# Turning the projected x with transposing DMAs instead of on TensorE, in a three-layer float32 kernel

## The chip, the cores and the metric

The kernel runs on one core of one Trainium2 chip. The metric is device microseconds (us) of one execution; the median of two runs of the kernel before is 728.64 us. PE is TensorE (matrix products), DVE is VectorE, ACT is ScalarE, POOL is GpSimd, SP is the engine that issues most DMAs.

## The reference

Three layers follow each other on 4 batches of 448 rows and 768 channels (12 heads of 64):

```
attn = sigmoid(q @ k.T / 8 - log(448)) @ v                 # per head
gate = sigmoid(causal 5-tap convolution of attn, by channel)
x    = (gate * (attn @ w_val)) @ w_out
h    = relu(x.T @ w_tok1) @ w_tok2                          # mixes rows, 448 -> 256 -> 448
u    = x + h.T
out  = u + relu(u @ w_ch1) @ w_ch2                          # 768 -> 1536 -> 768
```

All of it is float32. The weights come as words of 64 bits (float64), which the kernel takes apart into a high and a low float32 part.

## The kernel before

**Numbers.** PE multiplies in a rounded float32 format. A matrix operand is therefore split into a high part (a rounding copy, on ACT) and a low part (the difference, on DVE), and each product is three: high by high, low by high, high by low. A *round* is 18 such products of 448 columns, six operand tiles by three.

**Stages.** First attention, for all 24 head pairs (`lead`), with the decoding of the first weights between (`dec_*`). Then the four batches, each in the steps that `dense_steps` lists: six *value rounds* (`pj(0, j)`: x by `w_val`; then the gate, and the split into `gv`), the *output stage* with six *output rounds* (`pj(1, j)`: `gv` by `w_out`, copied to `x2T`), and the token mixing. Token mixing needs x with rows on the partitions, but `x2T` has channels there: `transp(j)` turns the tile of 128 channels with four products by the identity (line 363, 448 rows being three and a half blocks of 128; the last 64 rows are doubled by line 355), and lines 365 to 368 split the result into `x2`. Three turned tiles make a half. `tok1(half, t)` (a *first token step*, 11 products) multiplies a half by `w_tok1`, `tok2(j)` (a *second token step*, 6 products) by `w_tok2`, adds x and stores u to `uscr` in HBM. Last the *channel stage*: four tiles of columns by twelve pieces of the hidden layer; `ch1(t, fc)` makes one piece (18 products into `psh`), `ch2` adds it into six accumulators (`pso`).

**Order.** The program is written in the order in which the engines' queues get it. `weave(steps, ops, share)` walks through PE's steps, which carry weights (products), and puts other work (`ops`) between them in proportion. The ops are: convolutions of the next batch (`post_ops`, which also reload x from `xscr` with `x_back`, on SP's queue, into four buffers), and the decoding of channel weights (`ch_ops`: eight steps for a piece, of DVE and ACT in turn, on loads by SP). Channel weights 2, 3 and 4 (`PRE`) are decoded early and parked in `wscr`; 0 and 1 are decoded in the last batch; 5 to 11 on DVE when the channel stage begins (`dec_ch`). Each engine works through its own queue in order; a waiting instruction holds up all that stand behind it.

**PSUM.** Projections, turned tiles and token steps share six tiles of one bank each (`psw`).

Of the kernel before, what the change touches and what calls it, by code (L numbers as in the profile page):

```python
# [12 lines left out]
U32 = mybir.dt.uint32  # L13
AF = mybir.ActivationFunctionType
# [4 lines left out]
PRE = (2, 3, 4)  # L19
CHAN_LOW = 600  # L20
OS_SHARE = 0.95
# [5 lines left out]
AHEAD = 5  # L27
SHIFT = 16
# [3 lines left out]
def tile_kernel(ctx, tc, qT, kT, v, w_val, conv_w, w_out, w_tok1, w_tok2, w_ch1, w_ch2, out):  # L32
# [69 lines left out]
    def decode_ops(pool, n, raw, h_out, l_out, sum_out=None, bufs=2):  # L102
        w = raw[:, : 2 * n].rearrange("p (n t) -> p n t", t=2)
        lo, hi = w[:, :, 0], w[:, :, 1]
        t = {}

        def first():
            t["a"] = pool.tile([P, DC], I32, tag="dec_a", bufs=bufs, name="dec_a")[:, :n]
            nc.vector.tensor_scalar(out=t["a"], in0=hi, scalar1=0x7FFFFE00, scalar2=None, op0=ALU.bitwise_and)  # L109
# [4 lines left out]
        def rest():  # L114
            t["c"] = pool.tile([P, DC], I32, tag="dec_c", bufs=1, name="dec_c")[:, :n]
            nc.vector.tensor_scalar(out=t["c"], in0=hi, scalar1=0x1FF, scalar2=None, op0=ALU.bitwise_and)
# [11 lines left out]
        def power():  # L128
            t["e"] = pool.tile([P, DC], I32, tag="dec_c", bufs=1, name="dec_e")[:, :n]
            nc.vector.tensor_scalar(out=t["e"], in0=t["a"], scalar1=-0x800000, scalar2=None, op0=ALU.bitwise_and)  # L130
# [11 lines left out]

        return [first, rebase, rest, join, sign, power, low, high]
# [148 lines left out]
    def x_back(i):  # L292
        x = xbp.tile([P, PAD + S], F32, tag="xb", bufs=4, name="xb")
        nc.gpsimd.memset(x[:, :PAD], 0.0)
# [30 lines left out]
    def dense_steps(b):  # L325
        gv, x2T, x2, h1 = {}, {}, {}, {}
        cur = {}

        def proj(sel, j, part):
# [16 lines left out]
            if sel == 0:  # L346
# [4 lines left out]
                split(gv[j][:, 0], gv[j][:, 1], g)  # L351
            else:
                x2T[j] = dn["late"].tile([P, 512], F32, tag="x2T", bufs=KD, name="x2T")
                nc.scalar.activation(out=x2T[j][:, :S], in_=ps[:, :S], func=AF.Copy)
                nc.vector.tensor_copy(x2T[j][:, S:], x2T[j][:, R0:S])

        def transp(j):
# [9 lines left out]
            nc.vector.tensor_tensor(  # L367
                out=x[REM:, NF], in0=pt[REM:, NF], in1=f(x[REM:, NF]), op=ALU.subtract
# [15 lines left out]
        def tok2(j):  # L384
# [11 lines left out]
            u = x2T[j][:, :S]  # L396
            nc.vector.tensor_tensor(out=u, in0=ps[:, :S], in1=u, op=ALU.add)
            nc.gpsimd.dma_start(uscr[b, j], u)

        def pj(sel, j):  # L400
            return [(12, lambda part=part: proj(sel, j, part)) for part in range(3)]

        def tr(j):
            return [(4, lambda: transp(j))]
# [8 lines left out]
        if b + 1 == B:  # L413

            outs = pj(1, 0) + pj(1, 1) + tr(0) + pj(1, 2) + tr(1) + pj(1, 3) + tr(2) + pj(1, 4) + pj(1, 5)

            outs = outs[: -len(pj(1, 5))]
            now = pj(1, 5) + t1(0, 0) + t1(0, 1) + tr(3) + tr(4) + tr(5)
            outs += [s + (True,) for s in now] + t2(0) + t2(1) + t2(2)
            return val, outs, t1(1, 0) + t1(1, 1) + [(18, lambda: ch1(0, 0))], t2(3) + t2(4) + t2(5)  # L420
        first = pj(1, 0) + pj(1, 1)
        if b == 0:

            first[2:4] = first[3], first[2]
# [114 lines left out]
    def post_ops(b):  # L539
        ops, gates = [], []  # L540
        for i in range(b * NP, (b + 1) * NP):
            parts = {}

            def first(i=i, parts=parts):
                parts["all"] = post_parts(i)
                parts["all"][0][0]()
                parts["all"][1]()

            ops.append(first)
            for t in range(1, KW):  # L550
                ops.append(lambda t=t, parts=parts: parts["all"][0][t]())
                if t == 2:
                    ops += gates
                    gates = [lambda parts=parts: parts["all"][3]()]

            def end(i=i, parts=parts):
                parts["all"][2]()
                if i + 4 < NPT:
                    x_back(i + 4)

            ops.append(end)
        return ops + gates
# [37 lines left out]
    def ch_parts(pool, fc, which, raw):  # L600
        if fc in PRE:
            to = [pool.tile([P, DM], F32R, tag=f"pre{a}", bufs=1, name="pre") for a in range(2)]
            ops = decode_ops(pool, DM, raw, *to, bufs=1)
# [9 lines left out]
        return decode_ops(pool, DM, raw, *wch[fc][which], bufs=1)  # L613
# [59 lines left out]
    def ch1(t, fc, lo=0, hi=KD):  # L673
# [12 lines left out]
        if (t, fc) == (0, 0):  # L686
# [24 lines left out]
    with tc.manual_schedule():  # L711
# [22 lines left out]
        back1, back2 = [], []  # L734
        for b in range(B):
            val, outs, t1, t2 = dense_steps(b)
            if b:

                weave(val[0] + back1 + sum(val[1:], []) + back2, first.pop(0), 0.95)
            else:  # L740
                val = sum(val, [])
                for n in (12, 8, 4):
                    val.insert(n, (0, dec_step))
# [7 lines left out]
            if b + 1 < B:  # L751
                weave(outs, post_ops(b + 1))
            else:
                os = outs + t1 + t2
            back1, back2 = t1, t2
            if b + 2 == B:
                pre.release()
                xbp.release()
                rp["a"] = tc.alloc_tile_pool(name="p2a", bufs=1, side="left")
                wch_alloc(rp["a"], 0)  # L760
# [82 lines left out]
```

## Time and profile before

| | |
|---|---|
| median of 2 runs | 728.64 us (728.64 to 728.65) |
| profiled execution, its own time | 728.47 us |
| its span, first to last instruction | 726.6 us |
| PE busy | 720.5 us, 99% of the span |
| DVE, ACT, POOL busy | 398.6, 256.4, 40.3 us |
| attention stage | until about 133 us |
| four batches | about 133 to 385 us |
| channel stage | about 385 to 726 us |

The share of an engine is a mean over stages: DVE is busy 55% of the span, but almost without a break in the output stages of the batches, where it does the convolutions of the next batch. Products are pipelined on PE, so the time of one (0.27 to 0.39 us) is longer than the step from one to the next (0.17 to 0.23); the chain of waits, which adds up in order of time, gives the second. A wait that another engine's row names is one on which the engine stood still; idle time of an engine that nobody waits for costs nothing.

### The profile page before, as it was taken

The numbers are of one execution on the slowest core, as the hardware profiler recorded it, in microseconds if no ns is written. First come the engines' busy times: TensorE is split into PE (matmuls) and PEld (weight loads), VectorE is DVE, ScalarE is ACT, GpSimd is POOL, SyncE is SP. The second block draws the span as 40 slices with busy tenths as digits, with TensorE's granted clock in tenths as the row PEclk, the third lists the DMA queues.
The fourth block names the chain that finished last, engine by engine and source line by source line (L and its number), as shares of the span: only waits on it lengthen the run. The fifth ranks groups of instructions, "written<-read, shape, count | busy, mean of one in ns | idle before, by whom it ended". The sixth has DMA issues, their size and how long they took to land.

```text
span 726.6 us, 10824 instructions
## 1 busy us (share of the span) xinstructions
PE 720.5 (99%) x4360; PEld 594.0 (82%) x4360; DVE 398.6 (55%) x690; ACT 256.4 (35%) x379; POOL 40.3 (6%) x90
## 2 busy tenths in 40 slices
PE   8999999999999999999999999999999999999998
PEld 3444444799999999999998888888888999999997
DVE  1799766489889879965577999220101400040002
ACT  5899888344333433422343443200001100020000
POOL 0001010000101111002012000000000000000000
PEclk9999999999999999999999999999999999999999
DMA  9747997221244233045827553240000600042001
GB/s 295 252 150 236 269 299 225 103 88 51 88 155 159 77 123 116 16 142 154 287 83 252 170 161 107 84 157 0 1 1 0 212 28 0 1 132 65 1 1 65
DMA packets 56737, 87.24 MB, mean 120 GB/s; under 512 B 8032, under 2 KB 48240, under 8 KB 56688
## 3 DMA queue, kind: packets, MB, share of 16 engines
q1 hardware_dynamic: 50352, 62.86, 28.0%
q0 software_dynamic: 5904, 23.23, 9.0%
q8 instruction: 34, 0.56, 0.3%
q10 hardware_dynamic: 432, 0.46, 0.2%
q14 instruction: 15, 0.12, 0.1%
HBM read 66.68 MB, written 19.86 MB: 119 GB/s over the span
## 4 chain that ended last, share of the span: by engine, by line
PE 91%; DVE 6%; ACT 1%; issue 1%; DMA 1%; SPq 0%; ACTq 0%
PE psh L680 24%; PE pso L701 24%; PE psd L340 18%; PE psy L277 8%; PE pss L262 8%; PE pst L380 4%; PE pst L393 3%; DVE gate L310 2%; PE pst L363 1%; DMA k<-kT 1%; ACT gv L87 0%; DVE dec_a L124 0%; DVE gate L349 0%; ACT ga L264 0%; DVE xs L318 0%
## 5 line engine op out<-in xcount | busy, mean ns | idle before, releaser
L89 DVE SCALAR_TENSOR_TENSOR r<-psh,r 128x384 fp32r<-128x384 f32 (+1 forms) x47 | 29.2, 621 | 214.5 <-ACT r L87 214.5
L680 PE MATMUL psh<-us,wch 128*128 128x512 f32 (+1 forms) x648 | 135.5, 362 | 0.0
L701 PE MATMUL pso<-r,wch 128*128 128x384 f32 (+1 forms) x630 | 131.1, 361 | 0.0
L680 PEld LDWEIGHTS psh<-us,wch 128*128 128x128 f32 x648 | 117.3, 188 | 12.7
L701 PEld LDWEIGHTS pso<-r,wch 128*128 128x128 f32 x630 | 113.8, 188 | 11.9
L87 ACT ACTIVATE r<-psh 128x384 fp32r<-128x384 f32 (+1 forms) x47 | 25.5, 542 | 231.6 <-PE psh L680 224.5
L340 PE MATMUL psd<-gv,wo 128*128 128x448 f32 x432 | 90.7, 365 | 0.0
L264 ACT ACTIVATE ga<-pss,bias_s 128x896 f32<-128x896 f32 x84 | 83.5, 1004 | 19.6 <-PE pss L262 18.9
L340 PE MATMUL psd<-xs,w 128*128 128x448 f32 x432 | 87.7, 362 | 0.1
L340 PEld LDWEIGHTS psd<-xs,w 128*128 128x128 f32 x432 | 80.8, 187 | 6.4 <-issue 0.7
L340 PEld LDWEIGHTS psd<-gv,wo 128*128 128x128 f32 x432 | 80.1, 188 | 5.1
L262 PE MATMUL pss<-q,k 64*64 64x448 f32 x672 | 78.6, 539 | 1.2 <-DMA k<-kT 0.7
L277 PE MATMUL psy<-ga,v 64*64 64x448 f32 x672 | 77.5, 536 | 0.0
L310 DVE SCALAR_TENSOR_TENSOR gate<-xb,cw,gate 128x448 f32<-128x448 f32 x96 | 65.7, 684 | 2.8
L262 PEld LDWEIGHTS pss<-q,k 64*64 64x64 f32 x672 | 26.2, 134 | 39.7 <-issue 29.2
L277 PEld LDWEIGHTS psy<-ga,v 64*64 64x64 f32 x672 | 25.7, 133 | 37.4 <-issue 35.9
L112 ACT ACTIVATE dec_a<-dec_a,exp_b 128x768 int32<-128x768 int32 (+3 forms) x43 | 36.8, 866 | 36.4 <-DVE dec_a L109 36.4
L124 DVE SCALAR_TENSOR_TENSOR dec_a<-raw,dec_a 128x768 int32<-128x768 int32 (+2 forms) x42 | 37.3, 888 | 19.6 <-ACT dec_a L112 19.6
L680 PE MATMUL psh<-us,w 128*128 128x512 f32 (+1 forms) x216 | 45.2, 362 | 0.0
L701 PE MATMUL pso<-r,w 128*128 128x512 f32 (+1 forms) x216 | 45.1, 362 | 0.0
L680 PEld LDWEIGHTS psh<-us,w 128*128 128x128 f32 x216 | 39.1, 188 | 4.3
L701 PEld LDWEIGHTS pso<-r,w 128*128 128x128 f32 x216 | 39.1, 188 | 4.2
(80 smaller groups left out, 648.0 us busy)
## 6 DMA issues: line engine op xcount, KB each, us to landing
raw<-w_ch SPq DMA_DIRECT2D x24, 768.0 KB, 4.3
v<-v SPq DMA_DIRECT2D x24, 224.0 KB, 5.9
uscr<-x2T POOLq DMA_DIRECT2D x24, 224.0 KB, 3.5
q<-qT SPq DMA_DIRECT2D x23, 224.0 KB, 3.9
k<-kT SPq DMA_DIRECT2D x22, 224.0 KB, 4.2
raw<-w_out POOLq DMA_DIRECT2D x6, 768.0 KB, 7.5
wscr<-pre POOLq DMA_DIRECT2D x12, 384.0 KB, 3.5
xscr<-xb SPq DMA_DIRECT2D x18, 224.0 KB, 4.4
```

Of the source, the lines that this page charges most:

```text
L87: nc.scalar.activation(out=h_out, in_=src, func=AF.Relu if relu else AF.Copy)
L89: nc.vector.scalar_tensor_tensor(out=l_out, in0=src, scalar=0.0, in1=f(h_out), op0=ALU.max, op1=ALU.subtract)
L112: nc.scalar.activation(out=t["a"], in_=t["a"], func=AF.Relu, scale=8.0, bias=exp_b)
L124: nc.vector.scalar_tensor_tensor(out=t["a"], in0=hi, scalar=-0x80000000, in1=t["a"], op0=ALU.bitwise_and, op1=ALU.bitwise_or)
L262: nc.tensor.matmul(ps[cols, j, :S], k[rows, keys], q[rows], start=True, stop=True)
L264: nc.scalar.activation(out=a, in_=ps[:, :, :S], func=AF.Sigmoid, bias=bias_s, scale=QK_SCALE)
L277: nc.tensor.matmul(y_t[i + h][cols, :S], v_t[i][rows, c, cols], a[rows, j], start=c == 0, stop=c == NB - 1)
L310: nc.vector.scalar_tensor_tensor(out=acc, in0=x[:, t : t + S], scalar=w, in1=acc, op0=ALU.mult, op1=ALU.add)
L340: nc.tensor.matmul(ps[:, :S], w(a, kk), s[:, c, :], start=kk == 0 and n == 0, stop=kk == KD - 1 and n == 2,)
L380: nc.tensor.matmul(ps[:, :HALF], a, x[:, m], start=n == 0, stop=n == len(mm) - 1)
L680: nc.tensor.matmul(ps[:, :n_t], wch[fc][0][a][:, kk * P : (kk + 1) * P], us_t[t, kk][:, c, :], start=kk == 0 and n == 0, stop=kk == KD - 1 ...
L701: nc.tensor.matmul(acc[j][:, :n_t], wch[fc][1][a][:, j * P : (j + 1) * P], r[c], start=fc == 0 and n == 0, stop=fc == KF - 1 and n == 2,)
```

## The change

- **Turning.** `transp` and its products go. `planes(j)` takes the 16-bit halves of each word of `x2T` apart with a copy on ACT, doubles the last 64 rows with a second one, and issues a transposing DMA on SP's queue, 128 x 1024 elements of 2 bytes from `pl` (three buffers) to `st` (one buffer). `join(j)` puts the halves together again with a copy on POOL, back into `pl`. `part2(j)` makes the high part in `x2` on ACT, `part3(j)` the low part on DVE. These four are steps of their own with weight 0, one to three rounds apart.
- **Token steps.** They move back: in the first three batches the three second token steps of the first half and both first token steps of the second half now stand behind the second value round of the next batch, one second token step behind its value rounds and the other two between its first output rounds. In the last batch two channel steps `ch1(0, 0)` and `ch1(0, 1)` stand among them, which write into two tiles of `wo`.
- **Gated values.** The low part (`low_gv`) is a step behind the third part of its value round, with room for another op between.
- **Convolutions** of the last two tiles of a batch go from the output stage to the next batch's value stage. The zeros ahead of a reloaded x are set by DVE, not POOL, and the reload stands two steps later.
- **Weights.** `PRE` is (2, 3); weight 4 is decoded with 5 to 11. Decoding uses the target or the raw data for its temporary values. Weights 0 and 1 are decoded from the last batch's value stage on, the loads of u and of weights 2 and 3 stand elsewhere in its steps.

```diff
-PRE = (2, 3, 4)
+PRE = (2, 3)
-OS_SHARE = 0.95
+OS_SHARE = 0.9
+EARLY = 2
+LATE = 2
...
-    def dense_steps(b):
+    def dense_steps(b, carry):
...
-                split(gv[j][:, 0], gv[j][:, 1], g)
+                nc.scalar.activation(out=gv[j][:, 0], in_=g, func=AF.Copy)
+                wait[j] = g
             else:
-                x2T[j] = dn["late"].tile([P, 512], F32, tag="x2T", bufs=KD, name="x2T")
-                nc.scalar.activation(out=x2T[j][:, :S], in_=ps[:, :S], func=AF.Copy)
-                nc.vector.tensor_copy(x2T[j][:, S:], x2T[j][:, R0:S])
-
-        def transp(j):
+                x2T[j] = dn["late"].tile([P, S], F32, tag="x2T", bufs=KD, name="x2T")
+                nc.scalar.activation(out=x2T[j], in_=ps[:, :S], func=AF.Copy)
+
+        def planes(j):
+            pl = dn["late"].tile([P, 2, 512], U16, tag="pl", bufs=3, name="pl")
+            st = dn["late"].tile([P, 2, NF + 1, P], U16, tag="st", bufs=1, name="st")
+            turn[j] = pl, st
+            nc.scalar.activation(
+                out=pl[:, :, :S], in_=x2T[j].bitcast(U16).rearrange("p (s h) -> p h s", h=2), func=AF.Copy
+            )
+            nc.scalar.activation(out=pl[:, :, S:], in_=pl[:, :, R0:S], func=AF.Copy)
+            nc.sync.dma_start_transpose(st.rearrange("p h c d -> p (h c) d"), pl.rearrange("p h s -> p (h s)"))
+
+        def join(j):
+            pl, st = turn[j]
+            back = pl.rearrange("p a b -> p (a b)")
+            nc.gpsimd.tensor_copy(back.rearrange("p (n h) -> p h n", h=2), st.rearrange("p h c d -> p h (c d)"))
+            turn[j] = back.bitcast(F32).rearrange("p (c d) -> p c d", c=NF + 1)
+
+        def part2(j):
...
-            pt = pd["pool"].tile([P, NF + 1, P], F32, tag="d", bufs=pd["n"], name="pst")
-            for c in range(NF + 1):
-                nc.tensor.transpose(pt[:, c], x2T[j][:, c * P : (c + 1) * P], ident)
             x = x2[half][:, :, jj * P : (jj + 1) * P]
-            nc.scalar.activation(out=x[:, : NF + 1], in_=pt, func=AF.Copy)
-            nc.vector.tensor_tensor(out=x[:, NF + 1 :], in0=pt[:, :NF], in1=f(x[:, :NF]), op=ALU.subtract)
+            nc.scalar.activation(out=x[:, : NF + 1], in_=turn[j], func=AF.Copy)
+
+        def part3(j):
...
+            raw = turn.pop(j)
+            nc.vector.tensor_tensor(out=x[:, NF + 1 :], in0=raw[:, :NF], in1=f(x[:, :NF]), op=ALU.subtract)
...
+        def low_gv(j):
+            nc.vector.tensor_tensor(out=gv[j][:, 1], in0=wait.pop(j), in1=f(gv[j][:, 0]), op=ALU.subtract)
...
-        outs = first + tr(0) + pj(1, 2) + tr(1) + pj(1, 3) + tr(2) + pj(1, 4)
-        outs += t1(0, 0) + t1(0, 1) + pj(1, 5) + tr(3) + t2(0) + tr(4) + t2(1) + tr(5) + t2(2)
-        return val, outs, t1(1, 0) + t1(1, 1), t2(3) + t2(4) + t2(5)
+        first = pj(1, 0) + tr(planes, 0) + pj(1, 1)
+        if b == 0:
+
+            first[2:5] = first[4], first[2], first[3]
+        def out(j, then):
+            steps = pj(1, j)
+            return steps[:1] + then + steps[1:]
+
+        outs = first + tr(planes, 1) + tr(join, 0) + carry[0]
+        outs += pj(1, 2) + tr(planes, 2) + tr(join, 1) + tr(part2, 0) + carry[1]
+        outs += out(3, tr(part3, 0)) + tr(planes, 3) + tr(join, 2) + tr(part2, 1)
+        outs += out(4, tr(part3, 1)) + tr(planes, 4) + tr(join, 3) + tr(part2, 2)
+        outs += out(5, tr(part3, 2)) + tr(planes, 5) + tr(join, 4)
+        outs += t1(0, 0) + t1(0, 1) + tr(part2, 3) + tr(part2, 4)
+        low, high = t2(0) + t2(1) + t2(2), t2(3) + t2(4) + t2(5)
+        both = tr(part3, 3) + tr(part3, 4)
+        end = tr(join, 5) + tr(part2, 5)
+        if last:
+            c = [[(18, lambda fc=fc: ch1(0, fc))] for fc in range(EARLY)]
+            rest = tr(join, 5) + c[0] + both + tr(part2, 5) + t2(0) + tr(part3, 5) + t2(1) + t2(2) + t1(1, 0) + t1(1, 1) + c[1] + high
+            return val, outs, rest
+        return val, outs, (both + end, tr(part3, 5) + low + t1(1, 0) + t1(1, 1), t2(3), (t2(4), t2(5)))
...
-                weave(val[0] + back1 + sum(val[1:], []) + back2, first.pop(0), 0.95)
+                early = val[0] + tok[0] + val[1] + tok[1]
+                rest = sum(val[2:], []) + tok[2]
...
-        for fc in range(CHAN_HELD + 1, KF):
+        for fc in range(CHAN_HELD, KF):
             dec_ch(fc)
```

Three places show how the instructions stand.

PE, end of the output stage of the first batch, before: `psd` is the sum of a projection, `gv` the gated values, `pst` a turned tile, `pst_2059` the sum of the first of the second token steps.

```order
L340 MATMUL psd<-gv,wo 128x448 x18
L363 MATMUL pst<-ident,x2T 128x128 x4
L393 MATMUL pst_2059<-wt2H,h_1989 128x448 x2
L393 MATMUL pst_2059<-wt2L,h_1989 128x448
L393 MATMUL pst_2059<-wt2H,h_2007 128x448 x2
L393 MATMUL pst_2059<-wt2L,h_2007 128x448
```

And with the change (`pst_2109` is that sum):

```order
L351 MATMUL psd<-xs,w 128x448 x36
L422 MATMUL pst_2109<-wt2H,h_2024 128x448 x2
L422 MATMUL pst_2109<-wt2L,h_2024 128x448
L422 MATMUL pst_2109<-wt2H,h_2039 128x448 x2
L422 MATMUL pst_2109<-wt2L,h_2039 128x448
```

The products by the identity are gone here and everywhere, and what stands ahead of the second token steps is no longer an output round but two value rounds of the next batch (`xs` by `w`).

SP's queue from the end of the first batch's value rounds on, before (`raw` are channel weights, `xb` reloaded x):

```order
L584 DMA raw_1781<-w_ch1 128x6x256
L589 DMA raw_1783<-w_ch2 128x1536
L295 DMA xb_1823<-xscr_61 128x448
L295 DMA xb_1867<-xscr_61 128x448
L295 DMA xb_1910<-xscr_61 128x448
```

And with the change:

```order
L634 DMA raw_1781<-w_ch1 128x6x256
L639 DMA raw_1783<-w_ch2 128x1536
L376 DMA_TRANSPOSE st_1827<-pl_1826 128x8x128
L376 DMA_TRANSPOSE st_1850<-pl_1849 128x8x128
L306 DMA xb_1862<-xscr_61 128x448
L376 DMA_TRANSPOSE st_1888<-pl_1887 128x8x128
L306 DMA xb_1912<-xscr_61 128x448
L376 DMA_TRANSPOSE st_1926<-pl_1925 128x8x128
```

The transposing DMAs stand between the reloads, in the same queue.

ACT where the channel stage begins, before (`dec_a` is the first decoding step on ACT, `wch5` and `w` the high part of a channel weight, `r` the high part of a channel step's result, `psh_4048` channel step 1, `psh_4093` channel step 2):

```order
L87 ACTIVATE wo_3807<-psh_3788 128x512
L141 ACTIVATE w_3492<-dec_a_3725 128x768
L112 ACTIVATE dec_a_3868<-dec_a_3868,exp_b_66 128x768
L87 ACTIVATE r_3860<-psh_4048 128x512
L141 ACTIVATE wch5_3857<-dec_a_3868 128x768
L112 ACTIVATE dec_a_3881<-dec_a_3881,exp_b_66 128x768
L87 ACTIVATE r_3859<-psh_4093 128x512
```

And with the change (`wo_3775<-psh_3756` is channel step 1, `psh_4063` channel step 2, `psh_4102` step 3):

```order
L90 ACTIVATE wo_3775<-psh_3756 128x512
L150 ACTIVATE w_3425<-dec_a_3711 128x768
L121 ACTIVATE dec_a_3833<-dec_a_3833,exp_b_66 128x768
L90 ACTIVATE r_3829<-psh_4063 128x512
L150 ACTIVATE wch4_3827<-dec_a_3833 128x768
L90 ACTIVATE r_3828<-psh_4102 128x512
```

The first weight decoded in the channel stage is now 4, and its first high part stands behind the result of channel step 2, where weight 5's stood behind that of step 1.

## Rows read from the trace of the kernel before

**Rows 1.** The page, its head and part 1: busy us (share) x instructions.

```profile
span 726.6 us, 10824 instructions
PE 720.5 (99%) x4360; PEld 594.0 (82%) x4360; DVE 398.6 (55%) x690; ACT 256.4 (35%) x379; POOL 40.3 (6%) x90
```

**Rows 2.** Waits of PE: who waited for whom, us in total, times, longest.

```profile
PE psi L724 <- DVE zero L713: 1.2, 1, 1.2
PE pss L262 <- DMA k<-kT: 0.7, 1, 0.7
PE pss L262 <- ACT ga L264: 0.5, 2, 0.4
```

**Rows 3.** Chain of waits in order of time, second batch on: start us, us, what.

```profile
191.12 3.82 PE pst L380 x22
...
212.94 3.60 PE pst L393 x18
...
223.75 0.44 PE pst L363 x4
224.19 3.61 PE psd L340 x18
...
364.97 1.31 PE pst L363 x12
...
373.71 4.12 PE psh L680 x18
...
385.54 4.08 PE pso L701 x18
...
463.06 4.08 PE psh L680 x18
```

**Rows 4.** Groups of instructions by line and form, whole span: busy us, mean ns.

```profile
L310 DVE SCALAR_TENSOR_TENSOR gate<-xb,cw,gate 128x448 f32<-128x448 f32 x96 | 65.7, 684 | 2.8
L124 DVE SCALAR_TENSOR_TENSOR dec_a<-raw,dec_a 128x768 int32<-128x768 int32 x36 | 34.4, 954 | 19.6 <-ACT dec_a L112 19.6
L93 DVE TENSOR_TENSOR gv<-gate,gv 128x448 fp32r<-128x448 f32 x24 | 15.0, 626 | 15.9 <-ACT gv L87 15.9
L349 DVE TENSOR_TENSOR gate<-psd,gate 128x448 f32<-128x448 f32 x24 | 14.9, 621 | 10.0 <-PE psd L340 10.0
L87 ACT ACTIVATE gv<-gate 128x448 fp32r<-128x448 f32 x24 | 13.9, 578 | 59.0 <-DVE gate L349 59.0
L365 ACT ACTIVATE x<-pst 128x512 fp32r<-128x512 f32 x24 | 13.5, 590 | 1.3 <-PE pst L363 1.3
L366 DVE TENSOR_TENSOR x<-pst,x 128x384 fp32r<-128x384 f32 x24 | 13.3, 554 | 2.5 <-ACT x L365 2.0
L354 ACT ACTIVATE x2T<-psd 128x448 f32<-128x448 f32 x24 | 13.1, 545 | 54.3 <-PE psd L340 54.3
L367 DVE TENSOR_TENSOR x<-pst,x 64x128 fp32r<-64x128 f32 x24 | 7.1, 294 | 0.5
L141 ACT ACTIVATE pre<-dec_a 128x768 fp32r<-128x768 f32 x6 | 5.0, 837 | 0.9 <-DVE dec_a L124 0.9
```

**Rows 5.** DMA issues: out<-in, engine, count, KB each, median us to landing.

```profile
xscr<-xb SPq DMA_DIRECT2D x18, 224.0 KB, 4.4
xb<-xscr SPq DMA_DIRECT2D x18, 224.0 KB, 2.5
...
out<-ur SPq DMA_DIRECT2D x12, 256.0 KB, 2.1
```

**Rows 6.** POOL's fills and its masked select, groups as in rows 4.

```profile
masks.py:199 POOL TENSOR_SCALAR_AFFINE_SELECT ident<-ident 128x128 f32<-128x128 f32 x1 | 0.3, 307 | 0.1
...
masks.py:197 POOL MEMSET ident<- 128x128 f32 x1 | 0.2, 206 | 0.0
...
L75 POOL MEMSET bias_s<- 128x1 f32 x1 | 0.1, 99 | 0.3 <-POOLq L832 0.3
```

**Rows 7.** Second batch's output stage: stretch, length, busy (x) by PE, PEld, DVE, ACT, POOL.

```profile
218.00:248.20 30.20, 30.20 (x166) 28.36 (x165) 28.10 (x56) 12.60 (x25) 3.75 (x11) 1.00 0.37 118
```

**Rows 8.** DVE in order of time: first and last step of late decoding.

```profile
391.03 0.56 DVE L109 TENSOR_SCALAR dec_a<-raw 128x768 int32<-128x768 int32 x1
...
451.08 0.96 DVE L133 SCALAR_TENSOR_TENSOR wch<-raw,dec_e 128x768 fp32r<-128x768 f32 x1
```

More of the change, by code (lines that the diff above doesn't have):

```diff
@@ L141, in high @@
                 nc.scalar.activation(out=h_out, in_=t["a"].bitcast(F32), func=AF.Copy)
+        if inside:
+            return [first, rebase, sign, rest, join, power, low, high]
         return [first, rebase, rest, join, sign, power, low, high]
@@ L612, in ch_parts @@
             wch_place(fc)
-        return decode_ops(pool, DM, raw, *wch[fc][which], bufs=1)
+        spare = lambda: rp["p"].tile([P, DC], I32, tag="dec_c", bufs=1, name="dec_c")
+        return decode_ops(
+            pool, DM, raw, *wch[fc][which], bufs=1, spare=spare if fc >= CHAN_HELD else None, inside=fc < CHAN_HELD
+        )
     def pre_load(fc):
@@ L733, in tile_kernel @@
             x_back(i)
[L734 removed]
+        tok, conv = None, []
         for b in range(B):
[L736 removed]
+            val, outs, after = dense_steps(b, tok[3] if b else ([], []))
             if b:
[L739 removed]
+                early = val[0] + tok[0] + val[1] + tok[1]
+                rest = sum(val[2:], []) + tok[2]
+                if b + 1 < B:
+                    ops = first.pop(0)
+                    n = len(PRE)
+                    both_ops = []
+                    for k in range(n):
+                        both_ops += conv[k * len(conv) // n : (k + 1) * len(conv) // n]
+                        both_ops += ops[k * len(ops) // n : (k + 1) * len(ops) // n]
+                    weave(early + rest, both_ops, 0.95)
+                else:
+                    weave(early, conv, 0.95)
+                    pre.release()
+                    xbp.release()
+                    rp["a"] = tc.alloc_tile_pool(name="p2a", bufs=1, side="left")
+                    wch_alloc(rp["a"], 0)
+                    held = ch_ops(rp["a"], [(fc, which) for fc in range(2) for which in range(2)])
+                    weave(rest, held[:16], 0.95)
             else:
                 val = sum(val, [])
[L742 removed]
+                for n in (16, 10, 5):
                     val.insert(n, (0, dec_step))
@@ L751, in tile_kernel @@
             if b + 1 < B:
-                weave(outs, post_ops(b + 1))
-            else:
[L754 to L760, printed above, removed]
-                first.append(ch_ops(rp["a"], [(0, 0), (0, 1)]))
-        for j in range(KD):
-            prep_load(0, j)
-        ops = ch_ops(rp["a"], [(1, 0), (1, 1)])
-        for fc in PRE[:2]:
-            pre_load(fc)
-        for j in range(KD):
-            ops.insert(3 * j + 2, lambda j=j: prep_split(0, j))
+                ops, conv = post_ops(b + 1)
+                weave(outs, ops)
+            else:
+                os = outs
+            tok = after
+        load = [lambda j=j: prep_load(0, j) for j in range(KD)]
+        cut = [lambda j=j: prep_split(0, j) for j in range(KD)]
+        ops = [load[0], load[1]]
+        for j in range(2, KD):
+            ops += [load[j], held[14 + j], cut[j - 2]]
+        ops += [held[20], cut[4], held[21], cut[5]] + held[22:24]
         weave(os, ops, OS_SHARE)
+        weave(tok, [lambda fc=fc: pre_load(fc) for fc in PRE] + held[24:], OS_SHARE)
         psw.release()
```

87 lines of the change are left out of this document (49 added, 38 removed).

## The prediction

> **What bounds the kernel now.** The page's first part comes first: PE is busy 720.5 of 726.6 us [rows 1]. PE's waits come next: the longest is 1.2 us, at the very start, and the others together are as long [rows 2]. So PE runs without a gap from the first product to the last, and the end moves only by work that leaves PE or by a gap that opens. The chain of waits then gives the price of each PE stage [rows 3]: a projection round (18 products) 3.61, the two first token steps 3.82, three second token steps 3.60, a channel step of 18 products 4.08 to 4.12. Between them stand four turning products for each of 24 tiles: 0.44 when one tile stands alone, 1.31 for the three that stand together in the last batch.
>
> **What leaves PE.** The order shows that the 96 turning products are the only PE work that goes; everything else is only moved. 21 x 0.44 + 1.31 = 10.55 us. Since PE waits for nothing, all of this is gain, as long as the new way of turning is done in time. That gives 728.47 - 10.55 = 717.9 for the profiled execution (its own time, 0.17 below the median of the runs), and nothing in the change can give more.
>
> **The new turn, and when it is due.** A tile now goes through two copies on ACT (`planes`), a transposing DMA on SP's queue, a copy on POOL (`join`), a copy on ACT (`part2`) and two differences on DVE (`part3`). The DMA's target `st` has one buffer, so the DMA of a tile waits for the `join` of the one before: six turns of a batch run one after another, and each takes the DMA + the join + two hand-offs, for which I take 0.1 each.
>
> ACT's copies: rows of 448 and 768 elements (0.545 and 0.837) [rows 4] give 0.91 ns an element, so 896 and 128 elements take about 0.95 and 0.25 us. With the copy from PSUM (0.545) a turn begins about 1.85 us after its round ends. After the last turn come 0.59 + 0.55 + 0.29 and hand-offs [rows 4], about 1.75.
>
> In the first batch the first round ends 4.8 us into the output stage (a third of the second round now stands ahead of its last third), so the chain of turns starts at 6.7. The first token step comes after six rounds, at 21.6, and the fourth tile's half is due 3.82 + 2 x 3.61 + 3.60 later, at 36.2. Less 1.75 that leaves 13.1 us for three turns and 27.8 for six: **4.4 and 4.6 us a turn**. In later batches the first round ends at 3.6 and the carried token steps give 2.4 more: (38.6 - 1.75 - 5.5)/6 = 5.2; the x reloads on the same DMA engines, each a transfer of 2.5 us, cost the second and third batch about 0.35 of it. The last batch has a channel step of 4.1 in place of two value rounds: 4.7.
>
> **What a turn takes.** No transposing DMA and no POOL copy is in this trace. *The DMA:* 256 KB. The nearest row is the reload of x, 224 KB on the same queue in the same stretch, 2.5 us [rows 5], which is 2.9 for 256 KB; a 256 KB store lands in 2.1, a 224 KB store in the busy attention stage in 4.4. I take 3.0, ends 2.1 and 4.4. The Trainium skill (Advanced Engine Details and Errata, section X-Bar Transpose (TRN2)) says that on this chip transposing DMAs are as fast as others; the reload's row would then hold. Another page of the Trainium skill (VectorE: DVE Perf Modes, section The three transpose paths) gives 1309 ns for one 128x128 block of two-byte elements; if the eight blocks of a turn followed one another at that, an estimated 10.5 us, the sum would be near 890 us. No run here shows either yet.
>
> *The join:* 1024 elements a partition. Filling 1 and 128 columns took 0.099 and 0.206, 0.84 ns an element, so 0.96 us at least; the masked select of 128 columns took 0.307, 1.64 ns an element, so 1.78 [rows 6]. A plain copy computes nothing and is nearer the fill: 1.1.
>
> *Behind the waits:* on SP the x reloads and weight loads queue behind a transposing DMA that waits for a join; on POOL the stores of u queue behind a join that waits for its DMA (nobody reads u before the last batch); on ACT the next copies out of PSUM and the gated values queue behind `part2`, but PE has six PSUM tiles and is not held at once.
>
> So a turn is 3.0 + 1.1 + 0.2 = **4.3 us**, against 4.4, 4.6, 4.85, 4.85 and 4.7. It fits, barely; by the ends it is 3.3 to 6.4. For single turns that meet a reload or a weight load on the DMA engines I add 1.0 us over the whole (0 to 24 x 0.35 would be the ends).
>
> **The other edits.** DVE is busy 28.1 of 30.2 us in an output stage [rows 7]; two of six convolutions (four steps of 0.684 us each, beside a first product) [rows 4] leave it for the next value stage, as does a small copy, so `part3` finds room. The memset that moves from POOL to DVE is under 0.1 each. Both cost nothing while PE is ahead of them. If DVE is late, the gated values are late next.
>
> *Value to output.* Three second token steps (3.6) stood between the last value round and the first output round, now one (1.2). The last gated value needs 0.621 + 0.578 + 0.626 and hand-offs, 2.1 us [rows 4]; its cover is now 1.2 and two thirds of a round, 2.4 us: 1.5 to spare. A decode step of 0.95 on DVE and one of similar length on ACT stand in its way (ACT's order puts a decode ahead of gated values). That costs 0 to 1.4 a batch; I take 1.3 in all, in the last batch, where most decode steps stand.
>
> *Channel weights.* Weight 4 is no longer decoded early but with 5 to 11, on DVE. Before, DVE worked on them from 391.03 to 452.0 [rows 8], 13 pieces of 4.69 us with the splits between (a first one stands before), and the first piece of weight 11 was ready one piece before the end, 15.7 us ahead of its step at 463.06 [rows 3]. Now two and a half more pieces lie behind the point where the decode first waits for a split (11.7 us), and in ACT's order the first high part of weight 4 stands behind the split of channel step 2, which ends 8.2 to 12.2 us after the first `pso` step, where before the decode went on 5.5 us after it: 3.4 to 7.4 later. 15.7 less 11.7 less that: from 0.6 to spare to 3.4 late. I take 1.0 late, below the middle, because in PE's order `ch2` products stand between the parts of the late channel steps and fill such a wait.
>
> **Sum.** -10.55 + 1.0 + 1.3 + 1.0 = -7.25: 721.2 for the profiled execution, **721.4 us** against the median of 728.64, 1.0% faster.
>
> **Rivals.**
> 1. *A turn is too long (slower side).* Place: the first token step of each half, waiting for `x`. Each us above the times due is paid six times a batch: 24c - 114 us for a turn of c. It eats the 7.25 + 1.0 from c = 5.1 on. At 5.5 (DMA 4.0, join 1.3) it gives 24 x 5.5 - 114 = 18 less 8.25: 738. At the upper end, 6.4, 760. For it: one buffer, no slack, and rows of 3.5 to 4.4 for such transfers under traffic. Against: the row nearest in place and kind says 2.5. Chance 0.27, of which 0.15 lies above 742.
> 2. *POOL and DVE hold each other up.* If a `join` cannot run while DVE reads two operands from SBUF (the convolutions, 0.684 us each, fill the output stage), it waits half of one, 0.35 us, and DVE loses 1.1 us for each of 24 joins. A turn is then 4.65: about 0.8 us lost in the first batch, and gated values late by about 1 in the other three: 725. The trace can't speak, since no POOL instruction of it reads SBUF. The Trainium skill states this very rule (SBUF — State Buffer, section Who interferes with whom): two SBUF inputs on VectorE and a GpSimd read exclude each other for the whole instruction. Chance 0.28.
> 3. *The gain goes to other waits.* The value-to-output hand-off costs 1.4 in every batch and the decode 3.4: 728.64 - 10.55 + 1.0 + 5.6 + 3.4 = 728.1. For it: cover cut from 6.0 to 3.6. Against: 1.5 us are still left. Chance 0.08.
>
> **Chances.** Forecast 0.37, and the three above. A measurement of this kernel can tell about 2% from no change, 14.6 us. No case reaches 714, since only 10.55 leave PE: faster 0.01. The forecast, rivals 2 and 3 and the near half of rival 1 lie within: 0.84. Slower 0.15. The range goes from all of the gain, 718, to 742, where 0.15 of rival 1 are left out.
>
> **What would show it.** Right: no turning products; PE's span of the four dense batches 10 us shorter; transposing DMAs landing in about 3.0 us, `join` at about 1.1; PE without a wait of more than 1 us at the first token step. If the DMA takes 4 us or more, PE's waits will name `x` from ACT or DVE at the first token step, and rival 1 holds. If `join` shows 1.5 us and more, or DVE's convolutions show 1 us and more beside it, rival 2. A wait of the first output round for gated values, or of a channel step for decoded weights, longer than 2 us would show rival 3.

## The result and the profile after

Two runs of the changed kernel gave 736.02 and 737.38 us, median **736.70** against 728.64: ratio 1.0111 [1.0067, 1.0154], 1.1% slower. 721.4 had been forecast. The profiled execution (736.02) has a span of 734.2, 7.6 more than before [rows 1]. Its page, head and part 1:

```profile
span 734.2 us, 10699 instructions
PE 717.7 (98%) x4264; PEld 586.4 (80%) x4264; DVE 411.3 (56%) x684; ACT 286.3 (39%) x427; POOL 68.4 (9%) x88
```

The 96 turning products are gone, yet PE's busy time fell by 2.8 us only and its idle time grew by 10.4. DVE issues six instructions fewer and is busy 12.7 us longer. The waits of PE, to be read against [rows 2]:

```profile
PE pst L409 <- ACT x L389: 6.2, 2, 4.6
PE pst L409 <- DVE x L395: 3.2, 3, 1.7
PE psi L777 <- DVE zero L766: 1.2, 1, 1.2
PE psd L351 <- ACT gv L362: 1.1, 1, 1.1
```

L409 is the first token step, so 9.4 us are waits for turned tiles. This is too little: PE's idle time counts from the end of the product before, and that end lies behind the point where the next one could start. The same waits in the rows of PE's weight loads:

```profile
PEld pst L409 <- ACT x L389: 7.6, 4, 5.0
PEld pst L409 <- DVE x L395: 4.9, 5, 2.0
```

That makes 12.5 us. By PE's rows, 7.9 of the 9.4 stand in two places; the rest is 0.8 in the second batch and 0.7 at the first half of the last. The first batch, in order of time, PE first, then POOL (the joins), DVE and ACT; the brackets give the idle time before and what ended it:

```profile
178.64 0.44 PE L409 MATMUL pst<-x,wt1H 128*128 128x384 f32 x1 [1.53 <-ACT x L389]
178.92 0.34 PE L409 MATMUL pst<-x,wt1L 128*128 128x384 f32 x1
180.99 0.99 PE L409 MATMUL pst<-x,wt1H 128*128 128x384 f32 x2 [1.73 <-DVE x L395]
```

```profile
174.54 1.49 POOL L381 COPY pl<-st 128x1024 uint16<-128x1024 uint16 x1 [2.87 <-DMA st<-pl]
178.97 1.60 POOL L381 COPY pl<-st 128x1024 uint16<-128x1024 uint16 x1 [2.94 <-DVE gate L321]
```

```profile
174.74 1.65 DVE L395 TENSOR_TENSOR x<-pl,x 128x384 fp32r<-128x384 f32 x1
176.41 0.29 DVE L396 TENSOR_TENSOR x<-pl,x 64x128 fp32r<-64x128 f32 x1
...
179.31 1.62 DVE L395 TENSOR_TENSOR x<-pl,x 128x384 fp32r<-128x384 f32 x1
```

```profile
176.78 0.95 ACT L372 ACTIVATE pl<-x2T 128x896 uint16<-128x896 uint16 x1 [1.75 <-issue]
...
177.98 0.61 ACT L389 ACTIVATE x<-pl 128x512 fp32r<-128x512 f32 x1
```

L395 takes 0.56 alone. Twice it starts 0.2 to 0.3 us into a join and ends 0.36 us behind it: 1.1 us lost each time. The third tile's join is over at 176.03, but its `part2` (ACT L389) comes at 177.98: it queues behind a plane copy that could not start before `part3` of the second tile left its buffer, at 176.70. Then its own `part3`, behind convolutions, runs into the next join.

The last batch, second half: SP's queue, POOL and PE.

```profile
368.43 0.39 SPq L634 DMA_DIRECT2D raw<-w_ch  x1
370.44 1.24 SPq L376 DMA_TRANSPOSE st<-pl  x1
```

```profile
347.98 1.36 POOL L381 COPY pl<-st 128x1024 uint16<-128x1024 uint16 x1 [7.14 <-DMA st<-pl]
...
369.06 1.35 POOL L381 COPY pl<-st 128x1024 uint16<-128x1024 uint16 x1 [4.16 <-DMA st<-pl]
375.89 1.32 POOL L381 COPY pl<-st 128x1024 uint16<-128x1024 uint16 x1 [5.48 <-DMA st<-pl]
```

```profile
377.92 0.69 PE L409 MATMUL pst<-x,wt1H 128*128 128x384 f32 x1 [4.64 <-ACT x L389]
```

The last transposing DMA leaves when the join before it is over, 2 us behind a load of 768 KB, and the join that waits for it starts 5.4 us later. From the first join to the sixth this batch needs 27.9 us, 5.6 a turn; in the first batch the first five joins stand 4.4 to 4.6 apart. The difference is in the DMAs: from issue to join they take 3.5, 3.8, 3.3, 4.1 and 5.4 us in these five turns, among loads of u, and 2.8 to 3.0 in those of the first batch.

Behind the waits in these two places TensorE ran at the lower clock. The windows (stretch, length, PE, PEld, DVE, ACT and POOL busy, granted clock, DMA share, GB/s):

```profile
180.90:184.00 3.10, 3.02 (x9) 3.02 (x10) 1.48 (x4) 1.26 (x2) 0.53 (x1) 0.52 0.38 85
377.90:382.30 4.40, 4.38 (x14) 4.29 (x15) 2.47 (x5) 1.39 (x2) 4.31 (x9) 0.50 0.87 235
```

A granted clock of 0.5 is 1.2 GHz. The products of 384 columns stand 0.32 us apart there and 0.17 elsewhere; with some 22 of them about 3.3 us are lost, which count as busy.

The channel stage loses a little too. The fourth channel step and the last products, before and after:

```profile
397.62 4.24 PE L680 MATMUL psh<-us,w 128*128 128x512 f32 x18
...
716.67 6.40 PE L701 MATMUL pso<-r,wch 128*128 128x384 f32 x36
```

```profile
403.89 4.24 PE L733 MATMUL psh<-us,w 128*128 128x512 f32 x18
...
724.31 6.41 PE L754 MATMUL pso<-r,wch 128*128 128x384 f32 x36
```

The lag grows from 6.27 to 7.64, by 1.4. So: -10.55 for the products, +12.5 waits at token steps, +3.3 lower clock, +1.1 gated value, +1.4 channel stage, +0.4 ahead of the first value product gives +8.15, where the span grew by 7.6; the difference of 0.5 is not placed.

The groups of the turn, and the convolutions (columns as in [rows 4]):

```profile
L321 DVE SCALAR_TENSOR_TENSOR gate<-xb,cw,gate 128x448 f32<-128x448 f32 x96 | 68.9, 718 | 2.7
L372 ACT ACTIVATE pl<-x2T 128x896 uint16<-128x896 uint16 x24 | 22.8, 948 | 9.1 <-DVE x L396 3.7 <-issue 3.1 <-ACT x2T L366 0.8
L395 DVE TENSOR_TENSOR x<-pl,x 128x384 fp32r<-128x384 f32 x24 | 19.8, 825 | 3.4 <-ACT x L389 3.3
```

And the instructions on `st` (ns min/median/max, first and last start), with the DMA's time to landing:

```profile
L381 POOL COPY pl<-st x24: 1317/1468/2081, 165.6 to 375.9; 128x1024 uint16<-128x1024 uint16 x24
...
DMA to landing us min/median/max: 2.7/3.2/5.9
```

### The profile page after: what moved, and what is told of

It reads as the page before. It is cut to its first block, busy times and chain, and to the rows that moved or that the text cites. A ratio compares the mean times of both kernels' runs of the same rounds, so it can differ in the third digit from the quotient of the medians.

```text
span 734.2 us, 10699 instructions
## 1 busy us (share of the span) xinstructions
PE 717.7 (98%) x4264; PEld 586.4 (80%) x4264; DVE 411.3 (56%) x684; ACT 286.3 (39%) x427; POOL 68.4 (9%) x88
## 4 chain that ended last, share of the span: by engine, by line
PE 78%; DVE 13%; ACT 3%; DMA 3%; issue 1%; POOL 1%; SPq 0%; ACTq 0%; DVEq 0%; POOLq 0%
PE psh L733 22%; PE pso L754 22%; PE psd L351 12%; PE pss L273 8%; PE psy L288 8%; PE pst L409 4%; DVE gate L321 2%; PE pst L422 2%; DVE raw L128 1%; DMA st<-pl 1%; DVE dec_a L133 1%; DVE x L395 1%; DVE gate L360 1%; DVE gv L430 1%; DVE x L396 1%
## 5 line engine op out<-in xcount | busy, mean ns | idle before, releaser
L351 PE MATMUL psd<-gv,wo 128*128 128x448 f32 x432 | 88.6, 362 | 1.2 <-ACT gv L362 1.1
L321 DVE SCALAR_TENSOR_TENSOR gate<-xb,cw,gate 128x448 f32<-128x448 f32 x96 | 68.9, 718 | 2.7
L381 POOL COPY pl<-st 128x1024 uint16<-128x1024 uint16 x24 | 35.9, 1498 | 136.4 <-DMA st<-pl 66.5
L133 DVE SCALAR_TENSOR_TENSOR dec_a<-raw,dec_a 128x768 int32<-128x768 int32 (+2 forms) x38 | 33.4, 880 | 21.5 <-ACT dec_a L121 21.4
L121 ACT ACTIVATE dec_a<-dec_a,exp_b 128x768 int32<-128x768 int32 (+3 forms) x39 | 33.0, 858 | 27.4 <-DVE dec_a L118 27.2
L409 PE MATMUL pst<-x,wt1H 128*128 128x384 f32 x112 | 33.7, 372 | 9.5 <-ACT x L389 6.2
```

The lines of the kernel that those rows point to most:

```text
L121: nc.scalar.activation(out=t["a"], in_=t["a"], func=AF.Relu, scale=8.0, bias=exp_b)
L133: nc.vector.scalar_tensor_tensor(out=t["a"], in0=hi, scalar=-0x80000000, in1=t["a"], op0=ALU.bitwise_and, op1=ALU.bitwise_or)
L321: nc.vector.scalar_tensor_tensor(out=acc, in0=x[:, t : t + S], scalar=w, in1=acc, op0=ALU.mult, op1=ALU.add)
L351: nc.tensor.matmul(ps[:, :S], w(a, kk), s[:, c, :], start=kk == 0 and n == 0, stop=kk == KD - 1 and n == 2,)
L381: nc.gpsimd.tensor_copy(back.rearrange("p (n h) -> p h n", h=2), st.rearrange("p h c d -> p h (c d)"))
L409: nc.tensor.matmul(ps[:, :HALF], a, x[:, m], start=n == 0, stop=n == len(mm) - 1)
```

## The experiments

Three theories were set against each other. **S**: turns stand in a row behind the one `st`. **H**: joins on POOL and instructions of DVE hold each other up. **D**: other transfers make transposing DMAs longer.

**Two `st` buffers.** Every other tile lands in a second buffer (in the last batch in a weight tile that is free until then).

```
-            st = ...tile([P, 2, NF + 1, P], U16, tag="st", bufs=1, ...)
+            st = (...tile([P, 2, NF + 1, P], U16, tag="st", bufs=1, ...), dn["st2"])[j % 2]
```

> The changed kernel with a second buffer for what the transposing DMA lands in (every other tile uses it), so that a DMA no longer waits for the join of the tile ahead. Theory S (the turns of a half stand in a row behind the one buffer): the waits of PE at the first token step of the first batch (1.53 + 1.73 us) and at that of the last batch's second half (4.64 us) go, and with them the matmuls at the lower clock behind them (about 1.3 and 2.2 us): 736.7 - 11.4 = 725, and up to 1.5 us less if the waits of 0.7 to 1.1 us go too. Theory H (a join on POOL and the two-operand instructions of DVE hold each other up): 24 joins still stand beside DVE, the third part of the turn is still held for 1 us, and the first batch keeps about half of its wait: 729 to 732. Theory D (other transfers make the last transposing DMAs 4 to 5.4 us long instead of 2.9): the last DMA leaves 7 us earlier, into the loads of u: 727 to 730.

Measured 731.84, ratio 1.004 [1.0028, 1.0053], 5 below the changed kernel. The wait of 4.64 in the last batch is down to 0.22, so S holds there. The first batch keeps 1.55 + 1.54: S is wrong for it. The last transposing DMA, now away 5 us earlier and 0.5 us behind the big load, takes 6.3 from issue to join (D). DVE's `tensor_scalar`, one operand, is held as well: POOL's and DVE's rows (0.45 is normal for L319):

```profile
167.95 1.59 POOL L381 COPY pl<-st 128x1024 uint16<-128x1024 uint16 x1 [0.59 <-DMA st<-pl]
```

```profile
168.24 1.54 DVE L319 TENSOR_SCALAR gate<-xb,cw 128x448 f32<-128x448 f32 x1
```

**Join on ACT**, one buffer.

```
-            nc.gpsimd.tensor_copy(back..., st...)
+            nc.scalar.activation(out=back..., in_=st..., func=AF.Copy)
```

> The changed kernel with the join on ACT instead of POOL; one st buffer as before. Theory H: nothing runs on POOL beside DVE any more, the convolution taps go back from 718 to 684 ns and the subtraction of the turn from 825 to about 555 ns; the first batch's wait falls from 3.3 us to under 1.5 and the time to 728 to 731. Theory S: the turn only gets shorter by the difference of the two joins (1.5 to about 1.1 us), which is some 0.4 us a turn; but ACT stands still while it waits for a DMA, and its evictions of the next product behind that: 733 to 738.

Measured 745.71, 1.0231 [1.0206, 1.0257]: slower than any theory said. DVE is as H says (busy 394.9; the taps, the steps of the convolutions, at 683 ns). But ACT stands still, once 8.5 us for one DMA in the last batch, with plane copies and copies out of PSUM behind it, and PE waits 13.2 us for `part2` there. Two groups, then POOL, SP's queue and ACT around that DMA:

```profile
L321 DVE SCALAR_TENSOR_TENSOR gate<-xb,cw,gate 128x448 f32<-128x448 f32 x96 | 65.6, 683 | 2.7
L381 ACT ACTIVATE pl<-st 128x1024 uint16<-128x1024 uint16 x24 | 32.7, 1361 | 14.8 <-DMA st<-pl 14.7
```

```profile
353.65 2.16 POOL L674 DMA_DIRECT2D w<-wscr  x4
```

```profile
354.60 1.25 SPq L376 DMA_TRANSPOSE st<-pl  x1
```

```profile
366.94 1.34 ACT L381 ACTIVATE pl<-st 128x1024 uint16<-128x1024 uint16 x1 [8.49 <-DMA st<-pl]
```

That DMA took 12.3 us. POOL, which has no joins to wait for here, issued four reloads of channel weights (384 KB each) 1 us ahead of it; in the changed kernel joins keep them back until 377. So D has a part in this loss too, and no run separates it from ACT's queue.

**PE turns x, all else as changed.**

```
         def join(j):
-            nc.gpsimd.tensor_copy(back..., st...)
+            for c in range(NF + 1):
+                nc.tensor.transpose(pt[:, c], x2T[j][:, c * P : (c + 1) * P], ident)
```

> The changed kernel with x turned by PE products as in the kernel before (24 x 4, a copy of 64 columns on DVE ahead of them), all else as changed: the steps of the token stage, the gated values' low parts a step later, the loads and the memset where the change puts them. If all the time lost belongs to the turning: PE gets its 10.5 us back, the waits at token steps (10 us and the slow clock behind them, 3.4 us) go: 736.7 + 10.5 - 14 = 733 at most, and 729 to 731 where the smaller losses go too, the time before. If the other edits cost something of their own (the gated values' hand-off, 1.1 us in the last batch; the weights of the channel stage late, 1.3 us), it stays 1 to 3 us above the time before: 730 to 732. If the other edits gain, it is below 728.

Measured 735.39, 1.0096 [1.0081, 1.0111]: 6.8 us above before, where 1 to 3 were expected. Not all of the loss belongs to the turning. PE's waits in this kernel:

```profile
PE psh L726 <- ACT wch L150: 1.5, 2, 0.9
...
PE psd L351 <- ACT gv L362: 1.0, 1, 1.0
PE ptr L374 <- DVE x2T L369: 1.0, 1, 1.0
...
PE psh L726 <- DVE wch L142: 0.7, 1, 0.7
...
PE pso L747 <- DVE r L92: 0.3, 1, 0.3
```

Channel weights that come late make 2.5, the gated value 1.0, the copy ahead of the turning products 1.0; this last is the experiment's own, since the changed kernel has no such copy on DVE. So the other edits cost at least 3.5 us here. Some 2 us are not placed.

**The same, weight 4 decoded early again.**

```
-PRE = (2, 3)
+PRE = (2, 3, 4)
```

> The kernel of the third experiment (the changed kernel, x turned by PE: 735.4, 6.8 above before) with the weights of channel step 4 decoded early again, as before the change. There PE waited 2.5 us for channel weights and for DVE behind their decode (ACT wch 1.5, DVE wch 0.7, DVE r 0.3). If decoding weight 4 among the late ones makes that: 735.4 - 2.5 = 732 to 733.5. If the decode is then missed elsewhere, because two pieces more (10 us of DVE) stand in the second and third batch beside the convolutions that the change puts off: waits of PE for DVE there, 735 to 742.

Measured 748.66, 1.0283 [1.0261, 1.0304]. No wait for channel weights is left, so weight 4 among the late ones makes those 2.5 us. In their place PE waits for gated values, up to 3.1 us at a time, in three batches:

```profile
PE psd L351 <- ACT gv L362: 9.7, 5, 3.1
PE psd L351 <- DVE gv L423: 1.4, 2, 1.1
```

So with PE turning the changed order of steps does not bear the early decode of weight 4: 13.3 us more.

**Join of 32 columns.**

```
-            nc.gpsimd.tensor_copy(back..., st...)
+            nc.gpsimd.tensor_copy(back...[:, :, :32], st...[:, :, :32])
```

> The changed kernel with the join cut to 32 of 512 pairs of columns (the rest of the turned tile stays what the planes held, scaled by a quarter so that all of it is finite: this kernel leaves the turning of x out). The DMAs and all waits between them stay. Theory S: each turn is shorter by some 1.3 us, so the third is 4 us earlier and the sixth over 5: the waits of 3.3 and 4.6 us at token steps go, 736.7 - 11.4 = 725. Theory H: the same, and DVE's instructions are short again: 722 to 725. Theory D: the last transposing DMA keeps its 5.4 us; the wait of 4.6 us shrinks to 2 or 3 us: 728 to 730.

Measured 724.1, 0.9939 [0.9922, 0.9956]. DVE's busy time is 395.2, 16.1 less than in the changed kernel: a join holds DVE up 0.67 us on average. Both waits of the first batch are gone, as S and H both say; this run does not tell the two apart. In the last one 2.3 us stay, with 5.8 us from issue to join for the last DMA, and they belong to D: D named 2 or 3 of them and a time too high, since the shorter joins saved more elsewhere.

**One load later.** The 768 KB stand behind the last transposing DMA on SP's queue.

```
+        raw40 = ld_ch(rp["a"], CHAN_HELD, 0)   # last in the hand-written order
...
-            for fn in ch_parts(rp["a"], fc, which, ld_ch(rp["a"], fc, which)):
+            raw = raw40 if (fc, which) == (CHAN_HELD, 0) else ld_ch(rp["a"], fc, which)
+            for fn in ch_parts(rp["a"], fc, which, raw):
```

> The changed kernel with one load moved: the 768 KB of channel weights that left at 368.4 us, 2 us ahead of the last transposing DMA on the same queue, now stands behind it. Theory D (that DMA took 5.4 us instead of 2.9 because of the load beside it): it lands in about 3.2 us, PE's wait of 4.64 us falls to about 2.4 and the stretch at the lower clock behind it gets shorter or goes: 732 to 735. Theory S alone (only the row of turns behind one buffer counts): the DMA and the wait stay, 736 to 737. A loss of 1 to 2 us is possible where the weights of that load are now due earlier than they are decoded.

Measured 733.65, 1.0067 [1.0052, 1.0082]: 3 below the changed kernel. SP, POOL and PE:

```profile
370.95 1.24 SPq L376 DMA_TRANSPOSE st<-pl  x1
372.28 0.53 SPq L634 DMA_DIRECT2D raw<-w_ch  x1
```

```profile
373.81 1.35 POOL L381 COPY pl<-st 128x1024 uint16<-128x1024 uint16 x1 [2.99 <-DMA st<-pl]
```

```profile
377.87 0.62 PE L409 MATMUL pst<-x,wt1H 128*128 128x384 f32 x2 [0.96 <-DVE x L395]
```

From issue to join it is 2.9 instead of 5.4, and 0.96 is left of 4.64. D holds for the last turn, as S does: either remedy removes that wait.

**The hold-up alone.** The kernel before, with a copy on POOL at each turn that nobody waits for.

```
+            nc.gpsimd.tensor_copy(junk..., x2T[j].bitcast(U16)...)
```

> The kernel before, with PE turning x, and 24 copies of 128x1024 two-byte elements on POOL added, one at each turn, which nobody waits for. Theory H: the copies take 1.35 to 2 us each and hold up DVE's instructions with two operands in SBUF, or wait for them: DVE's busy time goes from 398.6 by 24 x 0.67 = 16 us to about 410 to 415, the convolution taps from 684 to 720 to 770 ns; the time from 728.6 to 730 to 733, as far as DVE has no time to spare. Without a hold-up: DVE's durations stay, 728 to 729.

Measured 734.16, 1.0073 [1.0056, 1.009]: **5.4 us for copies without a reader**, above the 730 to 733 that H gave. The page's part 1, the taps and PE's wait at the token step, which the kernel before does not have:

```profile
PE 724.2 (99%) x4360; PEld 595.0 (81%) x4360; DVE 411.3 (56%) x690; ACT 256.3 (35%) x379; POOL 73.6 (10%) x114
```

```profile
L311 DVE SCALAR_TENSOR_TENSOR gate<-xb,cw,gate 128x448 f32<-128x448 f32 x96 | 73.2, 763 | 2.8
```

```profile
PE pst L385 <- DVE x L371: 3.2, 2, 2.1
```

DVE loses 12.7 us, 0.53 a copy, and the turn, although on PE, is late in the first two batches, by 2.1 and 1.0.

**Two buffers and later token steps.** In the first three batches the first half's first token steps stand one value round (18 products) later.

```
-        outs += t1(0, 0) + t1(0, 1) + tr(part2, 3) + tr(part2, 4)
+        half = t1(0, 0) + t1(0, 1) + tr(part2, 3) + tr(part2, 4)
...
-        return val, outs, (both + end, ...
+        return val, outs, (half + both + end, ...
```

> Two st buffers, as in the first experiment (731.8), and in the first three batches the token steps of the first half stand one value product (18 products of PE, 3.6 us) later, in the next batch. The waits there were 1.55 + 1.54 us in the first batch, 0.60 and 0.68 in the next two, with 0.3 to 1 us around them. If they come from the turn being late by less than 3.6 us (the held-up DVE, theory H), they go: 731.8 - 4.4 to 5.5 = 726.5 to 727.5, faster than before by a little. If what is late moves along (DVE has no time to spare in the batches, and the next hand-off waits in its place), they come back at the second half's steps or at the value products: 729 to 732.

Measured 726.3, 0.9963 [0.9948, 0.9978]: a little faster than before. Behind the first batch's output stage 0.96 at value rounds and 1.20 at a token step are left, for DVE; the gated value's wait in the last batch is gone.

**And in the last batch that load and the splits of u later.**

```
-            ops += [load[j], held[14 + j], cut[j - 2]]
+            ops += [load[j], held[14 + j]] + cut[max(j - 3, 0) : j - 2]
```

> The kernel of the experiment with two st buffers and later token steps, and in the last batch the load of channel weights behind the last transposing DMA and the splits of u for the channel stage one step later, behind the copies of the planes. In that batch the first transposing DMA took about 6 us and the last 6.3 beside other loads, and the second plane copy stood 3 us behind a split of u that waited for its load. If these make PE's waits in the last batch (1.09 + 1.05 us at its first token step, with 0.5 us of lower clock): 1 to 2.5 us below the kernel without these moves. If DVE's held-up third part makes them: no difference (within 0.5 us).

Measured 724.95, 0.9951 [0.9934, 0.9967]: 1.35 below, inside what was expected, but the intervals of the two overlap. The waits in question have not gone either: at the last batch's first token step PE waits 1.45 us, where it waited 1.57, and the last DMA, now ahead of the big load but right behind loads of u, takes 5.5 from issue to join. This step by itself stays open.

**And the joins of the first batch on ACT.**

```
+            if b == 0:
+                nc.scalar.activation(out=back..., in_=st..., func=AF.Copy)
+            else:
                 nc.gpsimd.tensor_copy(back..., st...)
```

> The fastest version so far (724.95: two st buffers, later token steps, late load and late splits of u), with the six joins of the first batch on ACT, the others on POOL. In that batch PE still waited 0.19 + 0.75 us at value products and 1.19 us at a token step, each for DVE (xs, x). Theory H: with no copy on POOL beside DVE there, its convolution taps and subtractions are all short (685 and 555 ns) and these 2.1 us go: 722.5 to 723.5. If ACT's own queue is the tighter one (it stands still until each DMA has landed): the waits come back under ACT's name, 725 to 728.

Measured **721.19**, 0.9898 [0.9882, 0.9915]: 1.0% faster than before. PE waits for nothing in the first three batches; its waits from the first value product on:

```profile
PE pst L414 <- DVE x L400: 1.0, 2, 0.6
...
PE psh L740 <- DVE wch L142: 0.5, 1, 0.5
PE psh L740 <- ACT wch L150: 0.3, 1, 0.3
```

H holds for the first batch: from 160 to 182 us DVE is busy 19.5 us instead of 21.4, and the 2.1 us of waits are gone. The other 1.7 of the 3.8 us gained lie mainly in the last batch, whose joins were not touched; why is not shown.

**All joins on ACT**, and **those of the first three batches**:

> The same fastest version with all 24 joins on ACT. With one st buffer the same move cost 9 us over the changed kernel, most of it one wait of 13 us for ACT in the last batch. If that was the row behind one buffer (theory S: the DMA waits for a join that waits in ACT's queue), two buffers take it away: 722 to 726, with no DVE instruction held up. If it is ACT's queue in the last batch itself (the splits of u, which wait for their loads, stand ahead of joins and plane copies): a wait of 4 us or more for ACT stays there, 728 to 735.

> The fastest version (721.2, joins of the first batch on ACT) with the joins of the second and third batch on ACT too, and only those of the last batch on POOL. PE waited for nothing in the second and third batch of that version (its waits of 0.65, 0.34, 0.53 and 0.27 us stand in the last batch and the channel stage). If the hold-ups there are covered: no difference, 720.5 to 722. If DVE freed there is ahead in the last batch: up to 1 us less. If ACT's queue becomes tight: waits for ACT at the token steps, 722 to 726.

Measured 730.27, 1.0026 [1.0016, 1.0035], and 721.82, 0.9908 [0.9891, 0.9924]. With all joins on ACT, PE waits 7.5 us for `part2` in the last batch, with two buffers as with one: `part2` stands in ACT's queue behind a join that waits for its DMA. That DMA took 7.2 us, and POOL's first four reloads had left at 345 us, 17 us earlier than with joins on POOL, so the queue and the traffic are not told apart here either. With the joins of the second and third batch on ACT nothing is gained; PE waits for no tile there either way.

## Why the prediction was wrong

*What leaves PE: right.* The products are gone, and once most waits were taken away 7.4 of their 10.55 us came out: 721.19 against a floor of 718. That it lies beside the forecast 721.4 is chance: it is another kernel, with a second buffer, later steps and joins on ACT.

*The DMA: right alone, wrong in company.* 3.0 was taken; it lands in 2.7 to 2.8 undisturbed and 3.2 in the median. So the Trainium skill's line (Advanced Engine Details and Errata, section X-Bar Transpose (TRN2)) agrees with this trace, where the 224 KB reload now takes 2.8. The 10.5 us worked out from another page of the Trainium skill (VectorE: DVE Perf Modes, section The three transpose paths) do not agree. The step that failed is the term "For single turns that meet a reload or a weight load on the DMA engines I add 1.0 us over the whole". In the last batch alone the turns took 27.9 us from first to last join where five at 4.4 take 22, with 5.4 us for the last DMA. PE paid 4.64 and about 2 of lower clock there; the sum has no term at all for the clock. That is rival 1's place and mechanism, by traffic and not by the turn as such.

*The join: wrong.* 1.1 was taken, from the fill; it takes 1.32 to 1.37 undisturbed, between the two ends, and 1.47 in the median. The turn in the first batch, whose DMAs met no traffic, is 4.4 to 4.6 instead of 4.3.

*After the last turn, "about 1.75": wrong.* Behind the first batch's third turn it took 5.2, from 176.03 to 181.25: 2.0 in ACT's queue behind a plane copy that waited for a `pl` buffer, 0.7 behind DVE's convolutions, 1.1 beside the next join, and 1.4 of its own work. The three `pl` buffers are in no step of the prediction; a fourth was not tried.

*DVE: the main step that failed.* "`part3` finds room" and "Both cost nothing while PE is ahead of them" hold for a DVE that keeps its pace, and joins take 0.53 to 0.67 us each from it. The sum puts nothing at this, and such copies alone cost 5.4 us in the kernel before. Rival 2 named it. It allowed 1.1 a join, too much, and 0.8 us for the first batch, too little: two waits of together 3.3 us and 1.4 of lower clock stood there, since in the first batch's output stage DVE has nothing to spare. The Trainium skill states the rule (SBUF — State Buffer, section Who interferes with whom): a VectorE instruction with two inputs in SBUF contends with a GpSimd instruction that reads SBUF, and the order of issue decides who blocks. Row by row the trace agrees: L395, begun inside a join, ends 0.36 us behind it, and a join that began 0.1 us into a DVE instruction of 0.95 took 2.08 us instead of 1.3. By the same section of the Trainium skill `tensor_scalar` can take part as well, and L319's 1.54 agrees. (That no POOL instruction before reads SBUF is not quite so: the masked select of [rows 6] reads `ident`, but at 2.1 us, where DVE is idle, so it shows nothing of this.)

*Value to output: right in size.* 1.3 was taken for the last batch, 1.1 came. *Channel weights: nearly right.* 1.0 was taken, 1.4 came, and 2.5 with PE turning. What was missed is how near the edge that order is: with two pieces of decoding more, and PE turning, it costs 13 us.

Rivals 1 and 2 both happened, rival 2 decisive in the first batch and rival 1 in the last. I gave each its chance as if the other were absent, and the sum of small slacks (0.1 us a turn in the first batch, 0.4 in the last) could not carry either.

## What to carry to other kernels

Moving work off the bound engine earns its time only if the new chain has slack of the size of its disturbances: here 4.3 against 4.4 was no fit but a coin toss, and one round later in PE's order was worth about 5 us. Price a copy on POOL by what DVE does beside it, not by its own time: copies that nobody read cost 5.4 us. Before a queue gets a transfer with a due time, look at what big load stands just ahead of it, and at what the other queues will issue once nothing holds them back.

## What the runs showed of the hardware

- A POOL copy of 128x1024 two-byte elements takes 1.32 to 1.37 us undisturbed and the same copy on ACT 1.36. A DVE instruction that begins inside one on POOL takes up to 1.1 us longer and ends 0.1 to 0.8 us behind it (a tap of 0.685: 1.83 at most, in the run with late splits of u).
- A transposing DMA of 256 KB lands in 2.7 to 2.8 us. Behind a load of 768 KB its join starts after 5.4 instead of 2.9; with loads of u and reloads of weights beside it, it took 12.3 once.
- The clock: after a wait of 4.64 us PE ran at 1.2 GHz for 4.4 us, and after two of 1.53 and 1.73 close together for 3.1; after single waits of 0.7 to 1.1 the 384-column products kept their 0.17 us spacing, and with joins on ACT a single wait of 2.9 in the first batch left the granted clock at 1.0. At 1.2 GHz these products stand 0.32 us apart, so here 7.9 us of waiting cost 3.3 more.
